# Blockwise causal attention and a gated FFN on one core: batch 2's q and k transposed between its v loads, its copies grouped, and one weight cast on VectorE

## The chip, the cores and the metric

The kernel runs on one core of one Trainium2 chip. The metric is the device time of one execution in microseconds; the median of several executions is compared. The profile is of one further execution, taken with the hardware profiler.

## The reference

Eight batches of eight heads, 576 positions, head width 64, all in float32. The attention is causal in blocks of 64 positions; its output, with the heads side by side, is the input of a gated feed-forward network (FFN).

```python
B, H, S, D = q.shape                      # 8, 8, 576, 64
scores = (1 / sqrt(D)) * (q @ k^T)
scores = where(row // 64 >= col // 64, scores, -1e9)
attn = softmax(scores)                    # over the keys
x = (attn @ v).transpose(0, 2, 1, 3).reshape(B * S, H * D)   # 4608 x 512
out = (relu(x @ w_gate) * (x @ w_val)) @ w_out               # d_ff = 1536
```

## The kernel before

Everything runs in bfloat16 with float32 sums. The 576 positions of a batch are split into 512 main positions and a tail of 64.

**Attention in rounds.** Round r is a pair of heads of one batch: batch r // 4, pair r % 4. A round multiplies keys with queries (`visit`, L378), exponentiates on ScalarE (L387, L393), sets the masked corners to zero by memset (`corners`, L686), multiplies with v for each head (`head_av`, `both_av`, L491), normalises on VectorE (L456, L457) and turns the result into xT, either by TensorE (`to_xT_pe`, L537, L538) or by a DMA transpose (`to_xT_dma`, L543). The tail of each batch is a round of its own kind (`tail_visit`, L412; `tail_av`, L471; its DMA transpose L485).

**The FFN as filler.** `ffn_gen` yields one matmul at a time: for each batch 96 products with w_gate and w_val (L568, with relu on ScalarE at L578 and the gating product hT on VectorE at L583) and 48 products with w_out (wo, L625, L645 to L659). One such matmul is one place, and 144 places are one batch. `run(base, events)` issues FFN matmuls up to each event's place and then the event. So events stand in a list, each with its place, and the order of every engine's instructions is the order in which the program issues them; there is no scheduler. Every engine and every DMA queue works in order. While the FFN of batch 0 runs (`run(0, ...)`) rounds 4 to 7 (batch 1) are interleaved with it; during the FFN of batch 1 (`run(144, ...)`) tail 0, rounds 8 to 11 (batch 2) and tail 1.

**Loading.** Float32 inputs go by DMA from the SP queue into a ring of ten `stage` buffers and are cast to bfloat16, mostly on GpSimd (called POOL in the profile): `cast_qk` (L168), `cast_v` (L181), `cast_v_chunks` (L189), `cast_tails` (L178), `cast_v_tail` (L195), weights in `cast_w` (L323). q and k must also be transposed. Batches 0 and 1 do that on TensorE (`pe_mains`, L238, copied out of the ffnp buffers of PSUM at L244; `pe_tails`, L256). Batches 2 and 3 do it by DMA: `transpose` (L209) turns one half (two pairs of heads) of q and of k into a `perm` buffer, and `unpermute` (L223) copies one pair from there into qTm (VectorE) and kTm (POOL), where `visit` reads it; their tails go by `transpose_tails` (L217). From batch 4 on, POOL's own DMA queue loads and casts in one step (`load_qkv`, L276).

**Buffers.** qTm, kTm, v_bf, qTt and kTt exist twice, by the parity of the batch, so batch 2 overwrites those of batch 0, which tail 0 reads last (kTm in its scores, v_bf in its products). The PSUM pool ffnp has three buffers; in the FFN of batch 0 the two output sums begun at place 96 hold two of them up to place 112.

Batch 2 before the change: its q and k are loaded first (`e2.load_qk`). At place 121 SP is given its v and its q and k tails (`load_2`), at 133 and 143 POOL casts a half of q and k and SP transposes it (`mains_2`), then come batch 2's v tail and batch 1's tails (`load_tails`). In the FFN of batch 1 the pairs are unpermuted at places 25, 45, 60 and 80, for rounds that begin at 41, 58, 75 and 92; `tails_2` at 32 casts both batches' tails on POOL and has SP transpose batch 2's, and `v_2` at 46 casts batch 2's v.

Of the kernel before, what the change touches and what calls it, by code (L numbers as in the profile page):

```python
# [17 lines left out]
def kernel(  # L18
# [88 lines left out]
    class Early:  # L107
# [46 lines left out]
        def load_tails(self, ts):  # L154
            both = new_stage(1024)
            for i, t in enumerate(ts):
                self.st["t", t] = both[0:64, 512 * i : 512 * i + 512]
                nc.sync.dma_start(
                    self.st["t", t].rearrange("p (h d) -> p h d", h=8),
                    (q, k, v)[t][self.b, :, 512:576, :].rearrange("h p d -> p h d"),  # L160
                )
# [156 lines left out]
    def load_w_out(i):  # L318
        return load_w(wo[i], moe_w_out, 512 * i)

    def cast_w(sts, eng):
        for dst, st in sts:
            eng(dst, st)  # L323
# [40 lines left out]
    def visit(r):  # L364

        b, hp = divmod(r, 4)
        at = attnT[r % 4]
        first = psum_sc.tile([128, 2, 512], FP, name="sc")
        second = psum_sc.tile([128, 2, 512], FP, name="sc")
        third = thirds()  # L370
        for c, hh in [(c, hh) for c in (2, 0, 1, 3) for hh in range(2)]:
            where = {
                0: first[:, hh, :],
                1: second[:, hh, 0:384],
                3: second[:, hh, 384:512],
                2: third[hh],
            }
            nc.tensor.matmul(  # L378
                where[c].rearrange("p (c n) -> p c n", n=128),
                kTm[b % 2][head_of(hh), c, hp, :],  # L380
                qTm[b % 2][head_of(hh), c:4, hp, :],
                start=True,
                stop=True,
            )

        def exp(sc, lo):
            return lambda: nc.scalar.activation(  # L387
                at[:, :, lo : lo + 512], sc, AF.Exp, scale=scale
            )

        def exp_third():
            for hh in range(2):
                nc.scalar.activation(  # L393
                    at[:, hh, 1024:1280], third[hh], AF.Exp, scale=scale
                )

        return exp_third, exp(first, 0), exp(second, 512)
# [44 lines left out]
    def corners(r, zero):  # L442

        at = attnT[r % 4]
        for lo, n in ((0, 512), (896, 128)):
            two = at[64:128, :, lo : lo + 2 * n].rearrange("p g (c n) -> p g c n", c=2)
            zero(two[:, :, :, 0:64])
# [52 lines left out]
    def head_av(r, hh):  # L500
        b, hp = divmod(r, 4)
        h = 2 * hp + hh
        at = attnT[r % 4]
        if hh == 0:
            xnats[r] = sb.tile([128, 4, 128], BF, name="xnat", bufs=3)
        xnat = xnats[r]
        if b > 0 or hh == 1:
            av = psum_ffn.tile([128, 4, 65], FP, name="ffnp")
        else:
            av = psum_one.tile([128, 4, 65], FP, name="one")  # L510
        products_with_v(b, h, at[:, hh, :], av)
        normalise(xnat[:, :, 64 * hh : 64 * hh + 64], av)

    def both_av(r):

        b, hp = divmod(r, 4)
        xnats[r] = sb.tile([128, 4, 128], BF, name="xnat", bufs=3)
        for hh in range(2):
            sc = psum_sc.tile([128, 2, 512], FP, name="sc")
            av = sc[:, 0, 0:260].rearrange("q (p e) -> q p e", e=65)  # L520
            products_with_v(b, 2 * hp + hh, attnT[r % 4][:, hh, :], av)
            normalise(xnats[r][:, :, 64 * hh : 64 * hh + 64], av)
# [160 lines left out]
    dve, act, pool = nc.vector.tensor_copy, nc.scalar.copy, nc.gpsimd.tensor_copy  # L683
# [7 lines left out]
    with tc.manual_schedule(engines={E.PE, E.DVE, E.Activation, E.Pool, E.SP}):  # L691
# [57 lines left out]
        e1, e2 = Early(1), Early(2)  # L749
        e1.load_qk(0, 4)  # L750
        ffn(23)
        w_out = [load_w_out(i) for i in range(2)]
# [11 lines left out]
        cast_w(w_out[0], pool)  # L764
        cast_w(w_out[1], pool)
        e1.cast_v(0, 4, pool)
        cast_w(w_out[2], pool)
        e1.cast_qk(4, 4, (pool, None))
        e1.cast_v(4, 4, pool)
        e0.cast_tails((pool, pool))  # L770
# [12 lines left out]
        def round_at(p, r, av, to_xT, after=(6, 13)):  # L783

            exps = []

            def begin():
                exps.extend(visit(r))
                exps[0]()
                exps[1]()  # L790

            return [
                (p, begin),
                (p + after[0], lambda: exps[2]()),
                (min(p + after[1], av[0] - 0.5), lambda: corners(r, zero_dve)),
                *(
                    [(av[0], lambda: both_av(r))]
                    if av[1] is None
                    else [(av[i], lambda i=i: head_av(r, i)) for i in range(2)]
                ),  # L800
                (to_xT[0], lambda: to_xT[1](r)),
            ]

        def tail_at(p, b, av):
            exps = []
            x = sb.tile([64, 512], BF, name="xtail", bufs=2)

            def begin():
                exps.extend(tail_visit(b))
                exps[0]()  # L810
                exps[1]()

            def end():
                tail_av(b, 1, x)
                tail_to_xT(b, x)

            return [
                (p, begin),
                (p + 6, lambda: exps[2]()),
                (av[0], lambda: tail_av(b, 0, x)),  # L820
                (av[1], end),
            ]
# [4 lines left out]
        early = {2: e2}  # L827

        def tails_2():
            e2.cast_tails((pool, pool))  # L830
            e2.transpose_tails()
            e1.cast_tails((pool, pool))
            e1.cast_v_tail(pool)

        def v_2():
            e2.cast_v_tail(pool)
            e2.cast_v_chunks(0, pool)
            e2.cast_v_chunks(1, pool)

# [9 lines left out]
        def mains_3(h0):  # L849
            early[3].cast_qk(h0, 4, (pool, pool))  # L850
            if h0 == 0:
                early[3].cast_tails((pool, pool))
# [7 lines left out]
        def un(b, hp, engs=(dve, dve)):  # L860
            return lambda: early[b].unpermute(hp, engs)

        def load_2():
            e2.load_v_chunks(0)
            e2.load_v_chunks(1)
            e2.load_tails((0, 1))

        def mains_2(h0):
            e2.cast_qk(h0, 4, (pool, pool))
            e2.transpose(h0 // 4)  # L870

        def load_tails():
            e2.load_tails((2,))
            e1.load_tails((0, 1))
            e1.load_tails((2,))

        events = round_at(96, 4, (112, 112.1), (116, pe_xT), (6, 11))
        events += round_at(104, 5, (120, 120.1), (127, pe_xT), (6, 15))
        events += round_at(126, 6, (138, 139), (146, pe_xT), (4, 9))
        events += round_at(137, 7, (148, None), (153, pe_xT), (3, 8))  # L880
        events += [
            (80, lambda: e1.cast_qk(0, 4, (None, dve))),
            (93, lambda: e1.pe_mains(0, (dve, act))),
            (95, lambda: e1.pe_mains(1, (dve, act))),
            (120.2, lambda: e1.cast_qk(4, 4, (None, act))),
            (121, load_2),
            (121.5, lambda: e1.pe_mains(2, (dve, act))),
            (123, lambda: e1.pe_mains(3, (dve, act))),
            (133, lambda: mains_2(0)),
            (142, lambda: e0.pe_tails((dve, act))),  # L890
            (143, lambda: mains_2(4)),
            (143, load_tails),
        ]
        run(0, events)
        events = tail_at(24, 0, (40, 44)) + tail_at(116, 1, (132, 136))
        for r, p in ((8, 41), (9, 58), (10, 75), (11, 92)):
            events += round_at(p, r, (p + 21, p + 25), (p + 25, to_xT_dma))
        events += [
            (100, lambda: e1.pe_tails((dve, act))),
            (20, lambda: store.pop()()),  # L900
            (32, tails_2),
            (25, un(2, 0, (dve, pool))),
            (45, un(2, 1, (dve, pool))),
            (46, v_2),
            (47, load_3),
            (60, un(2, 2, (dve, pool))),
            (62, lambda: mains_3(0)),
            (80, un(2, 3, (dve, pool))),
            (81, lambda: early[3].transpose(0)),
            (82, lambda: mains_3(4)),  # L910
            (101, lambda: early[3].transpose(1)),
# [6 lines left out]
        for b in range(3, B):  # L918
            events = tail_at(120, b, (136, 140))
# [43 lines left out]
```

## Time and profile before

| | us |
|---|---|
| Median of 4 runs (lowest, highest) | 373.39 (373.06, 375.13) |
| The profiled execution's own time | 376.17 |
| Its span, from the first to the last instruction | 374.3 |
| TensorE (PE) busy | 358.4, 96% of the span |
| VectorE (DVE) busy | 172.3, 46% |
| ScalarE (ACT) busy | 169.4, 45% |
| GpSimd (POOL) busy | 111.3, 30% |
| SP and ACT DMA queues, busy share of 16 engines | 44.0%, 7.9% |
| Mean granted TensorE clock | 0.991 of full speed |

Times in the profile are microseconds from the span's start. A line such as "PE one L378 <- POOL kTm L223: 3.3, 1, 3.3" says that TensorE's instructions of line 378 that write the tile `one` waited for POOL's writing of kTm at line 223, in total, how often, and the longest. In a timeline a line has its start, its length, engine, source line, operation, output<-input and shapes, and in brackets the idle time before it and what ended it. The stretches give for each window its length and each engine's busy time (with the number of instructions), then the granted clock, the DMA share and GB/s. Consecutive matmuls overlap in the trace, as their ends are modelled.

### The profile page before, as it was taken

To read this page: it belongs to the slowest core of one execution; us is meant where nothing else is said; L and a number is where in the kernel's file an instruction comes from. 1 tells how busy PE (TensorE), PEld (TensorE's weight loads), DVE (VectorE), ACT (ScalarE), POOL (GpSimd) and SP (SyncE) were. 2 spreads that over 40 slices of the span, in tenths; PEclk is the share of its full clock that TensorE was granted. 3 is DMA by queue.
4 is the path that set the end of the run, shared out by engine and by line. 5 is a ranking of instruction groups with operands and counts; after the bars stand their busy time and mean duration, and the time that the engine had idled before them with its cause. 6 is when DMAs were issued, how large, how long until landed. Compare 5 with 4: busy or idle time off the path is not lost.

```text
span 374.3 us, 7466 instructions
## 1 busy us (share of the span) xinstructions
PE 358.4 (96%) x2963; PEld 177.6 (47%) x2963; DVE 172.3 (46%) x398; ACT 169.4 (45%) x278; POOL 111.3 (30%) x142
## 2 busy tenths in 40 slices
PE   6899989869999999899999999999999999999996
PEld 2644544424555545344554545444544454444443
DVE  4744555434555553355335542554345444323432
ACT  4833755545426672355445534653366423302310
POOL 5765636257059940850048003000000000000000
PEclk9999999987999999999999999999999999999999
DMA  8999999959979999998669965957400330020004
GB/s 254 293 349 360 297 264 304 204 138 268 174 151 93 120 123 191 163 130 125 116 95 136 118 136 92 64 62 151 79 17 14 44 100 7 0 86 28 0 33 109
DMA packets 145188, 51.35 MB, mean 137 GB/s; under 512 B 124545, under 2 KB 139137, under 8 KB 145153
## 3 DMA queue, kind: packets, MB, share of 16 engines
q1 hardware_dynamic: 83616, 34.62, 44.0%
q0 software_dynamic: 56256, 7.08, 41.5%
q10 hardware_dynamic: 5280, 9.18, 7.9%
q8 instruction: 23, 0.38, 0.5%
q14 instruction: 13, 0.10, 0.1%
HBM read 37.75 MB, written 9.44 MB: 126 GB/s over the span
## 4 chain that ended last, share of the span: by engine, by line
PE 74%; DMA 15%; SPq 5%; POOL 2%; issue 1%; DVE 1%; ACT 1%; POOLq 0%
PE ffnp L568 42%; PE ffnp L625 21%; DMA stage<-in_moe_w_val_dram 5%; PE ffnp L491 4%; DMA stage<-in_moe_w_out_dram 4%; DMA stage<-in_q_dram 3%; PE sc L378 3%; DMA xT<-xnat 2%; PE ffnp L471 2%; SPq L139 2%; SPq L209 2%; PE one L378 1%; DMA stage<-in_k_dram 1%; PE sc L412 1%; POOL wo L323 1%
## 5 line engine op out<-in xcount | busy, mean ns | idle before, releaser
L583 DVE TENSOR_TENSOR hT<-gate_sb,ffnp 128x512 bf16<-128x512 bf16 x106 | 72.7, 686 | 91.9 <-PE ffnp L568 78.6
L578 ACT ACTIVATE gate_sb<-ffnp 128x512 bf16<-128x512 f32 x108 | 64.7, 601 | 105.3 <-PE ffnp L568 105.2
L568 PE MATMUL ffnp<-xT,wg 128*128 128x512 bf16 x384 | 104.8, 382 | 2.2 <-DMA xT<-xnat 1.4
L625 PE MATMUL ffnp<-wo,hT 128*128 128x512 bf16 (+1 forms) x444 | 102.0, 373 | 1.1 <-POOL wo L323 1.0
L568 PE MATMUL ffnp<-xT,wv 128*128 128x512 bf16 x376 | 101.4, 382 | 0.0
L568 PEld LDWEIGHTS <-wg 128*128 128x128 bf16 x432 | 40.5, 98 | 48.0 <-issue 4.9
L568 PEld LDWEIGHTS <-wv 128*128 128x128 bf16 x432 | 40.2, 98 | 46.4 <-issue 3.4
L625 PEld LDWEIGHTS <-hT 128*128 128x128 bf16 x444 | 40.7, 98 | 42.6 <-issue 1.9
L387 ACT ACTIVATE attnT<-sc 128x1024 bf16<-128x1024 f32 x56 | 57.0, 1040 | 0.0
L659 DVE COPY ob<-ffnp 128x512 f32<-128x512 f32 (+1 forms) x35 | 23.7, 676 | 40.5 <-PE ffnp L625 40.5
L276 POOL DMA_DIRECT2D v_bf<-in_v_dram x20 | 16.8, 880 | 69.0 <-PE ffnp L471 69.0
L491 PEld LDWEIGHTS <-attnT 128*128 128x128 bf16 x640 | 26.7, 99 | 14.7 <-DVE xnat L457 3.3
L456 DVE RECIPROCAL recip<-ffnp 128x4 f32<-128x4 f32 (+1 forms) x73 | 13.1, 179 | 39.6 <-PE ffnp L491 27.8
L393 ACT ACTIVATE attnT<-one 128x256 bf16<-128x256 f32 x28 | 10.7, 382 | 38.5 <-PE ffnp L378 35.6
L491 PE MATMUL ffnp<-v_bf,attnT 128*128 128x65 bf16 x570 | 27.0, 195 | 0.0
L457 DVE TENSOR_TENSOR xnat<-ffnp,recip 128x256 bf16<-128x256 f32 x57 | 24.2, 424 | 2.0
L378 PEld LDWEIGHTS <-kTm 64*128 64x128 bf16 x224 | 9.4, 95 | 19.9 <-issue 12.3
L433 ACT ACTIVATE attnTt<-one 64x256 bf16<-64x256 f32 x8 | 3.0, 377 | 33.0 <-PE ffnp L412 33.0
L378 PE MATMUL sc<-qTm,kTm 64*128 64x512 bf16 (+1 forms) x168 | 17.5, 312 | 0.0
L424 ACT ACTIVATE attnTt<-sc 128x1024 bf16<-128x1024 f32 x16 | 15.6, 1016 | 0.0
L276 POOL DMA_DIRECT2D k_bf<-in_k_dram x16 | 14.3, 930 | 1.5 <-DMA v_bf<-in_v_dram 1.1
L276 POOL DMA_DIRECT2D q_bf<-in_q_dram x16 | 14.4, 956 | 0.0
(86 smaller groups left out, 256.8 us busy)
## 6 DMA issues: line engine op xcount, KB each, us to landing
out_dram<-ob ACTq DMA_DIRECT2D x32, 256.0 KB, 2.4
stage<-in_moe_w_gate_dram SPq DMA_DIRECT2D x6, 512.0 KB, 9.0
stage<-in_moe_w_val_dram SPq DMA_DIRECT2D x6, 512.0 KB, 8.9
stage<-in_q_dram SPq DMA_DIRECT2D x6, 512.0 KB, 6.9
stage<-in_k_dram SPq DMA_DIRECT2D x6, 512.0 KB, 7.3
stage<-in_moe_w_out_dram SPq DMA_DIRECT2D x6, 512.0 KB, 8.8
stage<-in_v_dram SPq DMA_DIRECT2D x20, 128.0 KB, 5.7
stage<-in_v_dram SPq DMA_DIRECT2D x8, 256.0 KB, 6.7
```

The source lines that it names most:

```text
L276: nc.gpsimd.dma_start(dst, src[b, :, 128 * c : 128 * c + n, :].rearrange("h p d -> p h d"),)
L378: nc.tensor.matmul(where[c].rearrange("p (c n) -> p c n", n=128), kTm[b % 2][head_of(hh), c, hp, :], qTm[b % 2][head_of(hh), c:4, hp, :], ...
L387: return lambda: nc.scalar.activation(at[:, :, lo : lo + 512], sc, AF.Exp, scale=scale)
L424: return lambda: nc.scalar.activation(at[:, :, 2 * i : 2 * i + 2, 0:256], main[i].rearrange("p g (h n) -> p g h n", h=2), AF.Exp, scale=scale,
L456: nc.vector.reciprocal(recip, av[:, :, 64])
L457: nc.vector.tensor_tensor(out=out, in0=av[:, :, 0:64], in1=recip.to_broadcast([rows, n, 64]), op=AX.mult,)
L491: nc.tensor.matmul(av[:, p, :], at[:, col : col + 128], v_bf[b % 2][:, c, h, :], start=(p == 0), stop=(c == p), skip_group_check=True,)
L568: nc.tensor.matmul(to, (wg, wv)[t][f // 4][:, c, 128 * (f % 4) : 128 * (f % 4) + 128], x[:, c], start=(c == 0), stop=(c == 3),)
L578: nc.scalar.activation(gate_sb, gate, AF.Relu)
L583: nc.vector.tensor_tensor(out=h, in0=gate_sb, in1=val, op=AX.mult)
L625: nc.tensor.matmul(op, hT[f][:, 128 * s : 128 * (s + 1)], wo[f // 4][:, f % 4, n0:n1], start=(f == lo), stop=(f == hi - 1),)
L659: nc.vector.tensor_copy(ob, op)
```

## The change

Four things change, all in the order of issue; every matmul, cast and transfer remains.

1. Batch 2's loads on SP. `load_2` is gone. `mains_2` loads two of the four v pieces, casts a half of q and k and transposes it, so that SP has: v 0, v 1, transpose q and k of half 0, v 2, v 3, transpose half 1, and then batch 1's tails and batch 2's tails. `mains_2(0)` comes at place 128 instead of 133.
2. Batch 2's copies. The pairs are unpermuted at places 25, 28, 52 and 56. `tails_2` comes at place 60, with batch 1's tails cast ahead of batch 2's; with it the transposes of batch 2's tails stand behind batch 3's loads (place 47) in SP's queue.
3. The second half of wo's last third is cast by VectorE at place 112.3 instead of by POOL.
4. In the FFN of batch 0 the transposes of batch 1 and rounds 4 to 7 are up to 5 places later, and round 4's two products with v stand a place apart.

```diff
-        cast_w(w_out[2], pool)
+        cast_w(w_out[2][:1], pool)
...
         def tails_2():
+            e1.cast_tails((pool, pool))
+            e1.cast_v_tail(pool)
             e2.cast_tails((pool, pool))
             e2.transpose_tails()
-            e1.cast_tails((pool, pool))
-            e1.cast_v_tail(pool)
+            e2.cast_v_tail(pool)
 
         def v_2():
-            e2.cast_v_tail(pool)
             e2.cast_v_chunks(0, pool)
             e2.cast_v_chunks(1, pool)
...
-        def load_2():
-            e2.load_v_chunks(0)
-            e2.load_v_chunks(1)
-            e2.load_tails((0, 1))
-
         def mains_2(h0):
+            e2.load_v_chunks(h0 // 4)
             e2.cast_qk(h0, 4, (pool, pool))
             e2.transpose(h0 // 4)
 
         def load_tails():
-            e2.load_tails((2,))
             e1.load_tails((0, 1))
             e1.load_tails((2,))
+            e2.load_tails((0, 1))
+            e2.load_tails((2,))
...
-        events = round_at(96, 4, (112, 112.1), (116, pe_xT), (6, 11))
-        events += round_at(104, 5, (120, 120.1), (127, pe_xT), (6, 15))
-        events += round_at(126, 6, (138, 139), (146, pe_xT), (4, 9))
-        events += round_at(137, 7, (148, None), (153, pe_xT), (3, 8))
+        events = round_at(101, 4, (113, 114), (117, pe_xT), (6, 11))
+        events += round_at(108, 5, (120, 120.1), (128, pe_xT), (6, 11.5))
+        events += round_at(128.5, 6, (139, 140), (146, pe_xT), (4, 9))
+        events += round_at(138, 7, (148, None), (153, pe_xT), (3, 8))
         events += [
...
-            (93, lambda: e1.pe_mains(0, (dve, act))),
-            (95, lambda: e1.pe_mains(1, (dve, act))),
+            (96, lambda: e1.pe_mains(0, (dve, act))),
+            (98, lambda: e1.pe_mains(1, (dve, act))),
+            (112.3, lambda: cast_w(w_out[2][1:], dve)),
...
-            (121, load_2),
-            (121.5, lambda: e1.pe_mains(2, (dve, act))),
-            (123, lambda: e1.pe_mains(3, (dve, act))),
-            (133, lambda: mains_2(0)),
+            (123, lambda: e1.pe_mains(2, (dve, act))),
+            (125.5, lambda: e1.pe_mains(3, (dve, act))),
+            (128, lambda: mains_2(0)),
...
             (143, lambda: mains_2(4)),
             (143, load_tails),
...
-            (32, tails_2),
             (25, un(2, 0, (dve, pool))),
-            (45, un(2, 1, (dve, pool))),
+            (28, un(2, 1, (dve, pool))),
             (46, v_2),
             (47, load_3),
-            (60, un(2, 2, (dve, pool))),
-            (62, lambda: mains_3(0)),
-            (80, un(2, 3, (dve, pool))),
+            (52, un(2, 2, (dve, pool))),
+            (56, un(2, 3, (dve, pool))),
+            (60, tails_2),
+            (66, lambda: mains_3(0)),
```

## The prediction

> **What bounds the kernel now.** I read the page first, its slices and its chain of waits: TensorE is busy for 96% of the span, so time can only come from the stretches in which it is not, or in which its clock is low.
>
> ```profile
> PE   6899989869999999899999999999999999999996
> PEclk9999999987999999999999999999999999999999
> ```
>
> A slice is 9.36 us. Counted from 0, the holes lie in slices 5 (47 to 56 us), 7 and above all 8 (75 to 84 us), and the clock is low in slices 8 and 9. Then the waits of TensorE (how long in total, how often, the longest):
>
> ```profile
> PE one L378 <- POOL kTm L223: 3.3, 1, 3.3
> PE ffnp L679 <- POOL ident masks.py:199: 1.6, 1, 1.6
> PE ffnp L568 <- DMA xT<-xnat: 1.4, 2, 1.0
> PE ffnp L471 <- DVE hT L583: 1.1, 1, 1.1
> PE sc L335 <- DVE kTm L244: 1.1, 2, 0.9
> PE ffnp L625 <- POOL wo L323: 1.0, 2, 0.7
> ```
>
> The first is round 9 waiting for its keys. The stretches around it (TensorE's busy us after the length, the granted clock third from the end):
>
> ```profile
> 76.00:78.00 2.00, 2.00 (x11) 0.90 (x10) 1.73 (x5) 1.46 (x2) 0.00 (x0) 1.00 0.82 169
> 78.00:80.00 2.00, 0.68 (x4) 0.10 (x1) 1.51 (x2) 0.02 (x1) 1.18 (x2) 1.00 0.25 44
> 80.00:82.00 2.00, 0.05 (x2) 0.06 (x4) 0.00 (x0) 0.00 (x0) 2.00 (x4) 0.80 0.26 46
> 82.00:84.00 2.00, 2.00 (x11) 0.70 (x12) 0.00 (x0) 1.57 (x3) 2.00 (x3) 0.50 0.67 237
> 86.00:88.00 2.00, 2.00 (x14) 1.01 (x13) 1.07 (x3) 0.00 (x0) 1.82 (x3) 0.50 1.22 201
> 88.00:90.00 2.00, 2.00 (x13) 0.82 (x13) 1.39 (x5) 0.60 (x1) 1.91 (x4) 1.00 1.09 348
> ```
>
> So the wait is paid twice: 3.27 us of idleness, and then a half clock until 88. Why the keys were late stands in the timeline of GpSimd and of the SP queue:
>
> ```profile
> 78.82 0.61 POOL L178 CAST q_bt<-stage 64x512 bf16<-64x512 f32 x1 [4.19 <-DMA stage<-in_q_dram]
> 79.38 0.97 POOL L178 CAST k_bt<-stage 64x512 bf16<-64x512 f32 x1
> 80.30 0.61 POOL L195 CAST v_bf<-stage 64x512 bf16<-64x512 f32 x1
> 80.86 1.03 POOL L223 COPY kTm<-perm 128x512 bf16<-128x512 bf16 x1
> ```
>
> ```profile
> 66.78 1.62 SPq L209 DMA_TRANSPOSE perm<-q_bf  x1
> 68.50 1.73 SPq L209 DMA_TRANSPOSE perm<-k_bf  x1
> 73.70 0.63 SPq L158 DMA_DIRECT2D stage<-in_q_dram  x1
> ```
>
> Round 9's kTm copy (80.86) was ready to run at 73.5, but GpSimd works in order, and ahead of it stood the casts of batch 1's tails, whose load SP issued only at 73.70, behind the four transposes. And VectorE stood 3.34 us at its first qTm copy (71.38) until the first transpose landed at 71.36, with hT L583 behind it, for which TensorE waited 1.13 us at 72.62.
>
> **The change part by part.** All sums are against the profiled execution, with a span of 374.3 us; its own time was 376.17 and the median of the four timed runs is 373.39, so a saving is taken over onto the median unscaled.
>
> *Transposes earlier (SP).* Ahead of the first transpose now stand two of batch 2's four v loads instead of four and two tail loads. In the trace SP began the third v load at 60.67, and the casts that the transposes read ended at 59.95 (q) and 61.43 (k), so the new wait of SP for GpSimd is at most some tenths; behind it stand v's second half, the second pair of transposes and all tails, none of which anyone waits for soon. Landing: a transpose took 3.1 to 4.6 us from issue to landing, a v load of the same queue up to 8.8, so q's lands between 64 and 69.5. I take 67.3: the second v load landed at 66.44, and two transposes that followed each other landed 0.9 to 1.3 apart. k's then lands at 68.2, against 72.28. The second pair has the same bytes ahead of it as before, less two tail loads: about 72 and 73 instead of 73.6 and 74.8.
>
> *First wait (1.13 us).* VectorE reaches the two grouped copies at about 69 (68.04 before, and 0.8 from the retimed stretch below); perm has landed. Two copies of 0.59 end at 70.2, where the one before ended at 71.97, so hT is ready before TensorE asks: gain 1.13, between 0.5 (transpose landing at 69.5) and 1.13. The copies now run beside GpSimd's two kTm copies. The rows show what that costs: the VectorE copy of 78.96 took 0.91 instead of 0.59 beside a cast on GpSimd, and that engine's next cast 0.97 instead of 0.61. With 0.3 more per copy VectorE is free at 70.8, still in time. [...]
>
> *Second wait (3.27 us).* Round 9's kTm copy now stands right behind round 8's, both once tail 0's scores (67.2 to 67.9 before) are done: two copies of 1.06 end near 71, and round 9 asks near 77.5. Gain 3.27. What is next late: round 8's products with v, four FFN products after round 9's scores, near 79.3. They need both v casts (1.03 each), which GpSimd does once tail 0's products have read the old v (75.66 before, 1.1 less now) and v's second half has landed; the fourth v load landed at 68.54 and now has two more transposes ahead, so near 71. That gives 76.6 for the casts: 2.7 us of room. Rounds 10 and 11 need the copies of the second pair, done by 79, and ask at 83 and 88. Batch 1's tails are cast at 79 to 81 and asked for past 90. Batch 2's own tails and their transposes move behind batch 3's loads; their first reader is tail 2, at 111.58: free. SP, without these two transposes (2.00 and 1.18 at 75.86) ahead of batch 3's loads, begins them near 77.5 instead of 80.49; behind the two in their new place wait only xT transposes of batch 2, read after 144.
>
> *Clock.* From round 9's begin to round 10's TensorE took 7.91 us (81.95 to 89.86) and for the same work from round 10 to 11 5.42 (89.86 to 95.28). If no long idle stretch is left, 2.49 us come back; at most 3.0 (half of the 6.05 us after 81.95). I take 2.5, since round 10's own small waits (0.23 at 92.29) will be round 9's too. The clock fell at 81.18, 2.5 us into the pause, and stayed at 0.5 for 6.83 us; the 1.03 us of idleness between 46 and 48 did not lower it. [...]
>
> *The earlier stretch, retimed (38 to 56 us).* Transposes of batch 1 and rounds 4 to 6 move 2 to 5 FFN places later, into places where the two sums of the output occupy two of three ffnp buffers. Following the instruction order with the trace's durations: the first output product waits for the last hT (0.69 of VectorE), 0.45; the fourth group of transposes shares one buffer with the third and waits for its copy (0.69 plus hand-over), 0.9; round 4's third score 0.2; round 4's first product with v waits for the memset that now stands behind the second output copy (0.69 + 0.30), 1.0. That is 2.55, against 0.24 + 0.31 + 0.73 and some 0.3 of shorter pauses that the trace shows there and that go or coincide (wo's last loads land at 45.54 and 46.87 either way). The later pauses of the stretch (0.27, 0.17 and shorter ones) about keep their sum. So +0.8, between 0 and 2. The DVE cast of wo's last piece takes 0.69 (VectorE's cast of the same shape at 36.56), ends near 48.6, where its reader now comes at 48.8: no wait; behind it wait the two reciprocals of round 4, in the 0.8. GpSimd is relieved of 1.04 us that lay before a cast waiting for its load: nothing.
>
> *Sum.* 1.13 + 3.27 + 2.5 − 0.8 = 6.1: a span of 368.2, and 367.3 on the median. After 96 us TensorE hardly waits in the trace, so the rest shifts as a whole; the 1.4 us of waits for xT near 153 stay, within a microsecond either way.
>
> **The rivals.**
> [...]
> (2) A new wait takes the old one's place: round 8's v casts or the second pair of copies end 1.5 us after TensorE asks, and the clock falls again: 1.5 + 2.5 back, 371.3. Against it is the 2.7 us of room.
> (3) Slower: the transposes in the middle of SP's queue hold up v's second half. SP works in order, and this load decides from the moment that its cast ends after 79.3: each microsecond later is one of TensorE's, plus 2.5 for the clock. It turns the whole slower once the load lands past 82, 11 us later than I put it: with 5 us of wait 7.5 are paid against 6.1 won, 374.8; with 7, 376.8. For it: landings of up to 8.8 us in this stretch.
> (4) The wait goes but the earlier stretch costs more than its upper bound, 3 us or more, without the clock: 369.5.
>
> **How the numbers follow.** Forecast 0.74 (its own range 365.5 to 369), rival 1 0.07, rival 2 0.06, rival 3 0.06, rival 4 0.07. Low end: earlier stretch free, the whole 3.0 of the clock, a part of xT's waits: 365. High end: into rivals 1 and 4, 370.2. About 0.5% (1.9 us) is what a measurement of this kernel can tell from no change: faster than 371.5 are the forecast, rivals 1 and 4 and most of 2, 0.91; a mix of rivals 1 and 2 falls within, 0.04; slower 0.05.
>
> **What would show it.** Right: no wait of PE L378 on POOL kTm, the clock at 1.00 from 76 to 90, the first L209 issue near 61, kTm copies of rounds 8 and 9 adjacent near 70, round 9's scores near 78. The earlier stretch: TensorE at FFN place 128 some 0.8 us later than the 55.0 of before. Wrong: a wait of L491 on POOL v_bf, or a clock of 0.50 anywhere between 40 and 100.

## The result, and the profile after

No change. The changed kernel took 374.37 us (median of 36 runs, 372.69 to 376.01); in the same comparison the kernel before took 373.72 (55 runs). The ratio is 1.0012, with a 95% interval of 0.9999 to 1.0025. The profiled execution of the changed kernel took 374.92 us with a span of 372.8, 1.5 less than the span of before. The forecast was 367.3 us, and its range ended at 370.2.

The waits of TensorE after the change, largest first (total, how often, longest):

```profile
PE ffnp L568 <- DMA xT<-xnat: 3.7, 1, 3.7
PE ffnp L679 <- POOL ident masks.py:199: 1.6, 1, 1.6
PE sc L335 <- DVE kTm L244: 1.1, 2, 0.9
PE ffnp L491 <- DVE attnT L686: 0.8, 1, 0.8
```

The wait for round 9's kTm is gone, and so is that for hT behind the first copies. In first place stands a wait of about the same size that before did not have: an FFN matmul waits for xT, the transposed output of attention. The page's slices show where it is (a slice is 9.32 us):

```profile
PE   6899989999969999999999999999999999999996
PEclk9999999999988999999999999999999999999999
```

The hole of slice 8 is filled. A new one stands in slice 11 (102 to 112 us), with the low clock beside it, in slices 11 and 12. The stretches show both places (length, busy time of PE, PEld, DVE, ACT and POOL, then the granted clock, DMA share, GB/s):

```profile
78.00:80.00 2.00, 2.00 (x22) 0.93 (x20) 1.97 (x3) 1.43 (x3) 2.00 (x3) 1.00 0.76 78
86.00:88.00 2.00, 2.00 (x19) 1.05 (x18) 1.34 (x4) 1.36 (x2) 0.00 (x0) 1.00 1.12 335
106.00:108.00 2.00, 0.18 (x14) 0.15 (x5) 0.14 (x1) 1.36 (x3) 1.61 (x2) 1.00 1.19 215
108.00:110.00 2.00, 0.14 (x1) 0.10 (x1) 0.00 (x0) 0.00 (x0) 0.26 (x1) 0.68 0.87 96
110.00:112.00 2.00, 2.00 (x6) 0.64 (x5) 0.00 (x0) 1.51 (x2) 2.00 (x3) 0.50 0.37 65
114.00:116.00 2.00, 2.00 (x7) 0.78 (x6) 0.32 (x1) 0.50 (x1) 2.00 (x4) 0.61 1.83 117
```

Between 76 and 90 TensorE is busy at full clock, as forecast. Between 106 and 110 it stands, and the clock then stays at one half until about 115.6. The pattern of 78 to 88 of the kernel before has come back 28 us later. Who is late is seen in the SP queue of the changed kernel and in the matmul that waits:

```profile
94.31 1.22 SPq L543 DMA_TRANSPOSE xT<-xnat  x1
95.62 1.27 SPq L209 DMA_TRANSPOSE perm<-q_bf  x1
96.97 1.38 SPq L209 DMA_TRANSPOSE perm<-k_bf  x1
98.45 3.49 SPq L543 DMA_TRANSPOSE xT<-xnat  x2
102.03 1.26 SPq L209 DMA_TRANSPOSE perm<-q_bf  x1
103.39 1.58 SPq L209 DMA_TRANSPOSE perm<-k_bf  x1
105.06 2.33 SPq L543 DMA_TRANSPOSE xT<-xnat  x1
```

```profile
109.86 0.59 PE L568 MATMUL ffnp<-xT,wg 128*128 128x512 bf16 x1 [3.68 <-DMA xT<-xnat]
```

The last L543 is round 11's xT. It was issued at 105.06 behind batch 3's second pair of q and k transposes (102.03, 103.39) and landed at 109.82; TensorE went on at 109.86. Before the change the queue looked like this:

```profile
100.53 1.27 SPq L209 DMA_TRANSPOSE perm<-q_bf  x1
101.89 1.29 SPq L209 DMA_TRANSPOSE perm<-k_bf  x1
104.66 1.19 SPq L543 DMA_TRANSPOSE xT<-xnat  x1
```

Between 103.18 and 104.66 SP stood there and waited for its data, which VectorE finished at 104.63; after the change it was ready at 98.48, and SP came to it 6.6 us later. The last writing of round 11's xnat, before and after:

```profile
104.21 0.42 DVE L457 TENSOR_TENSOR xnat<-ffnp,recip 128x256 bf16<-128x256 f32 x1
98.06 0.42 DVE L457 TENSOR_TENSOR xnat<-ffnp,recip 128x256 bf16<-128x256 f32 x1
```

Before the change the transfer landed at 109.3. Its first reader is the fourth matmul of batch 2's FFN (place 291: the four matmuls of a sum read the four pairs of heads in turn, and round 11 is the last pair), which ran at 112.27: 3.0 us of room. After the change this matmul was due 6.1 us earlier, at 106.18 (109.86 less the wait), and SP, without a pause of over 1.8 us from 77 to 105, issued the transfer 0.4 us later than before; it landed 0.5 later. That is the wait: 6.1 − 3.0 + 0.5 = 3.6.

The ledger, by the start of scores in the two traces (us; "lead" is how much earlier the changed kernel is):

| | before | after | lead |
|---|---|---|---|
| tail 0 | 67.30 | 67.81 | −0.51 |
| round 9 | 81.95 | 78.26 | 3.69 |
| tail 1 | 102.69 | 96.38 | 6.31 |
| tail 2 | 111.70 | 105.55 | 6.15 |
| round 12 | 118.79 | 119.17 | −0.38 |
| round 16 | 153.57 | 152.77 | 0.80 |
| end of span | 374.3 | 372.8 | 1.5 |

So 6.15 us were won, and 6.53 were given back between tail 2 and round 12: 3.68 of waiting, and 2.85 of FFN work at half clock. Between round 12 and the end 1.9 came back, all of it from 145 to 162 us, where the changed trace has none of the 1.4 us of waits for batch 3's xT.

### The profile page after: what moved, and what is told of

It is laid out like the page before. It is cut to its first block, busy times and chain, and to the rows that moved or that the text cites. A ratio compares the mean times of both kernels' runs of the same rounds, so it can differ in the third digit from the quotient of the medians.

```text
span 372.8 us, 7469 instructions
## 1 busy us (share of the span) xinstructions
PE 358.4 (96%) x2963; PEld 176.9 (47%) x2963; DVE 173.6 (47%) x399; ACT 169.5 (45%) x278; POOL 111.6 (30%) x141
## 4 chain that ended last, share of the span: by engine, by line
PE 77%; DMA 16%; SPq 2%; ACT 1%; POOL 1%; issue 1%; DVE 0%; ACTq 0%; POOLq 0%
PE ffnp L568 43%; PE ffnp L625 22%; DMA stage<-in_moe_w_gate_dram 5%; PE ffnp L491 4%; DMA stage<-in_k_dram 3%; PE sc L378 3%; DMA stage<-in_moe_w_out_dram 2%; PE ffnp L471 2%; DMA stage<-in_v_dram 2%; SPq L139 2%; DMA perm<-k_bf 1%; PE one L378 1%; DMA xT<-xnat 1%; PE sc L412 1%; ACT attnTt L424 1%
```

## The experiments

Theory A: round 11's xT is late only because of its place in the SP queue, behind transposes that nobody needs so soon; take it out of there and the gain appears, up to the next thing that is late. Theory B: the transfers of this stretch are too many whatever their order, and TensorE waits near 106 us in any case. The kernels of one comparison ran with the kernel before on the same chip; each ratio is against that.

**e1: batch 3's second pair behind round 11's xT.**

```diff
-            (101, lambda: early[3].transpose(1)),
+            (117.5, lambda: early[3].transpose(1)),
```

> The changed kernel with one edit: batch 3's second pair of q/k transposes on SP (L209, issued at 102.03 and 103.39 in the changed kernel's profile) goes behind round 11's xT (issued at 105.06, landing at 109.82, TensorE asking at 106.2). Theory A (the 6.1 us are lost because round 11's xT stands on SP behind loads and transposes that nobody needs sooner, plus the half clock of 6.83 us): xT of round 11 lands near 106, the 3.68 us wait of L568 goes to under 1, tail 2 begins near 105.4 and the next place 6 us sooner. Then the next late thing is batch 3's xT (landing near 151 behind batch 4's transposes, which TensorE would now ask for near 146), so by A the whole is between 368 and 373, with a wait on xT near 146 to 150. Theory B (the DMA engines move so much there that order does not matter): the wait of about 3.7 us stays near 106, time as the changed kernel, 374.

371.98 us (before 373.47), ratio 0.9954 [0.9915, 0.9992]. Round 11's xT is now the last of three that SP issues in one row, at 101.64, and it landed at 104.47:

```profile
98.03 4.83 SPq L543 DMA_TRANSPOSE xT<-xnat  x3
102.96 1.26 SPq L209 DMA_TRANSPOSE perm<-q_bf  x1
```

From tail 2's scores to round 12 the trace has 7.09 us, exactly as in the kernel before (after: 13.62). The wait near 106 has gone with the order alone, so theory B falls. But the next thing is late at once, the xT of batch 3:

```profile
145.86 0.38 PE L568 MATMUL ffnp<-xT,wg 128*128 128x512 bf16 x1 [0.19 <-DMA xT<-xnat]
147.66 0.38 PE L568 MATMUL ffnp<-xT,wg 128*128 128x512 bf16 x1 [0.77 <-DMA xT<-xnat]
149.24 0.49 PE L568 MATMUL ffnp<-xT,wg 128*128 128x512 bf16 x1 [1.21 <-DMA xT<-xnat]
```

These are 2.2 us, and the clock fell beside them for 3.4 us (149.4 to 152.8).

**e2: round 11's xT by TensorE.** The DMA is left out, and four matmuls transpose instead.

```diff
-            events += round_at(p, r, (p + 21, p + 25), (p + 25, to_xT_dma))
+            events += round_at(
+                p, r, (p + 21, p + 25), (p + 29, pe_xT) if r == 11 else (p + 25, to_xT_dma)
+            )
```

> The changed kernel with round 11's xT made by TensorE's transposes and a VectorE copy instead of the DMA transpose; nothing else moves. Theory A: no wait for xT near 106 at all, clock 1.00 from 100 to 120, and the wait reappears at batch 3's xT (near 146), where 2 to 5 us of it are paid: 368 to 372. Theory B: TensorE waits as long for round 10's xT (landing at 103.5) or another DMA by 110: 374.

373.16 us, ratio 0.998 [0.9951, 1.0009]: by itself not to be told from before, and outside theory A's 368 to 372. The profiled run (371.96 us) has no wait near 106 either, as theory A says, and 1.6 us for batch 3's xT.

**e3: the copy alone.** The kernel before, in which only round 9's copies are moved.

```diff
-            (45, un(2, 1, (dve, pool))),
+            (28, un(2, 1, (dve, pool))),
```

> The kernel before with one part of the change: batch 2's second pair unpermuted at place 28 instead of 45, so its kTm copy stands on POOL ahead of the tails' casts; SP's queue as before. If the copies' order alone were what paid: the 3.27 us wait of round 9 and the half clock go, 368. By my reading of the traces the tails' casts (waiting for a load that lands at 78.7) still stand ahead of the two v casts on POOL, so round 8's products with v wait from about 80.5 to 83.4 instead, and the clock falls all the same: 372.5 to 374.

372.07 us, ratio 0.9967 [0.9941, 0.9993]: this one line gains about 1.2 us, where the whole change gains nothing. It moves the wait on to the casts of v:

```profile
PE ffnp L491 <- POOL v_bf L189: 2.0, 2, 1.3
```

The 2.0 us come as 1.34 and 0.67, and here the clock did not fall, which had been expected otherwise. In the listed runs it hardly fell at all: the mean granted clock was 0.999 or 1.000 in six of seven.

**e4: the xT of rounds 11, 13, 14 and 15 by TensorE.** As e2, and for batch 3:

```diff
-                events += round_at(p, r, (p + 20, p + 24), (p + 24, to_xT_dma))
+                events += round_at(
+                    p,
+                    r,
+                    (p + 20, p + 24),
+                    (p + 28, pe_xT) if b == 3 and i else (p + 24, to_xT_dma),
+                )
```

> The changed kernel with the xT of rounds 11, 13, 14 and 15 made by TensorE instead of by DMA (16 transposes more on TensorE, about 4 x 0.22 us). Theory A: both waits on xT (near 106 and near 146) are gone and what is left is at most the wait of round 16 for its DMA-transposed q and k (landing near 147.5): 367.5 to 370. Theory B: the time stays within 1 us of the changed kernel's, the waits moving to other transfers.

369.77 us (four runs), ratio 0.9906 [0.9884, 0.9928], as theory A says, and no wait for an xT in the whole trace. Its largest waits:

```profile
PE ffnp L679 <- POOL ident masks.py:199: 1.6, 1, 1.6
PE ffnp L238 <- ACT k_bf L168: 1.3, 1, 1.3
```

**e5: the early stretch alone.** The kernel before with parts 3 and 4 of the change (wo's last cast on VectorE, rounds 4 to 7 later), without parts 1 and 2.

```diff
-        events = round_at(96, 4, (112, 112.1), (116, pe_xT), (6, 11))
+        events = round_at(101, 4, (113, 114), (117, pe_xT), (6, 11))
...
+            (112.3, lambda: cast_w(w_out[2][1:], dve)),
```

> The kernel before with only batch 0's retimed early stretch and wo's last piece cast by VectorE; batch 2's loads and copies stay in their old places. Theory A (SyncE's order decides): the retiming makes TensorE 0.5 us later at place 128, and that lag is swallowed in front of tail 1, where TensorE waits for kTm anyway; span and time as before, 373 to 374.4 us, with the wait for kTm about 3.3 us minus nothing and the slow clock beside it. Theory B (the retimed stretch is worth something of its own, or costs it): 0.8 us or more slower, 374.5 or over, or 0.8 faster.

374.48 us (before 373.47), ratio 1.0004 [0.9972, 1.0036]. The time lies between the ranges of the two theories. Neither a gain nor a loss over 0.4% comes from there. Theory A's wait of 3.3 us did not come, as the waiting moved: for hT 2.5 us instead of 1.1, for kTm 0.7 instead of 3.3.

**e6: the change without the early stretch.** The changed kernel with those same lines as before.

```diff
-        events = round_at(101, 4, (113, 114), (117, pe_xT), (6, 11))
+        events = round_at(96, 4, (112, 112.1), (116, pe_xT), (6, 11))
...
-            (112.3, lambda: cast_w(w_out[2][1:], dve)),
```

> The changed kernel with the early stretch and wo's last cast as in the kernel before: only batch 2's loads and copies are moved. Theory A: TensorE is some 0.5 us earlier from place 128 on and waits that much longer for round 11's xT, which SyncE's queue sets: 3.7 to 4.3 us near 106 us and the slow clock there; time as the changed kernel's, 373.5 to 375. Theory B (the retiming costs what the move wins): the time falls by 1 us or more, to 373 or less, with no wait over 1 us near 106.

374.10 us, ratio 1.0016 [0.9983, 1.0048]; the wait is nearly as large as in the changed kernel, not larger as theory A had it, and in the profiled execution the clock did not fall. The time shows that the retiming did not eat the gain:

```profile
111.53 0.38 PE L568 MATMUL ffnp<-xT,wg 128*128 128x512 bf16 x1 [3.25 <-DMA xT<-xnat]
```

**e7: e2's edit on the kernel before.**

> The kernel before with round 11's xT transposed by TensorE instead of a DMA; nothing else. Theory A (round 11's xT is late only once the rest is 6 us earlier): nothing is won, 373.0 to 374.0 us, the wait for kTm and the slow clock beside it stay. Theory B (this transfer held up the kernel before as well, or taking a transpose from SyncE helps whatever else waits): 372.5 or less.

374.40 us, ratio 1.0007 [0.9983, 1.0032]: nothing won (the time is 0.4 above theory A's range). Round 11's xT held up nobody before.

**e8: e1's line and rounds 13 to 15 by TensorE, on the changed kernel.** Its diff is that of e1 with that of e4 for batch 3.

> The changed kernel with batch 3's second pair of q and k transposes put behind round 11's xT in SyncE's queue, and the xT of rounds 13 to 15 transposed by TensorE. Theory A: no wait for an xT anywhere, round 11's landing about 104.5 us; 368.5 to 370 us, at or below the run that gave the xT of rounds 11, 13, 14 and 15 to TensorE (369.8). Theory B (the later pair makes batch 3's own tails late): a wait for batch 3's q or k over 1 us, 371 or more.

370.50 us, ratio 0.9911 [0.9879, 0.9944]; no wait for an xT, and batch 3's later pair is not waited for. It lies 0.5 above the expected 370 and cannot be told from e4, whose interval overlaps.

**e9 and e10: why batch 3's xT is late.** In e1 these three took 9.4 to 10.3 us from issue to landing, where round 11's took 2.8. While they were queued, SP issued batch 4's two long transposes (L286, 5.1 and 6.1 us each), and GpSimd, which has nothing that holds it back, issued its loads of batch 5 from 123 us on. Both kernels start from e1 and put a memset of a later round on GpSimd ahead of those loads: round 15's in e9, round 16's in e10.

```diff
-                (min(p + after[1], av[0] - 0.5), lambda: corners(r, zero_dve)),
+                (
+                    min(p + after[1], av[0] - 0.5),
+                    lambda: corners(r, zero_pool if r == 15 else zero_dve),
+                ),
```

> The kernel of e1 (batch 3's second pair of transposes behind round 11's xT), and round 15's masking memset on GpSimd, so that GpSimd's loads of batch 5, which stand behind it, start near 135 us instead of 123. Theory A (the next late thing, batch 3's xT, lands 8 to 10 us after its issue because SyncE's long transposes of batch 4 and these loads share the DMA engines between 123 and 136): the two L286 transposes issue in under 4 us instead of 5.1 and 6.1, batch 3's xT land earlier, the wait of 2.2 us for them falls under 1 us; 369.5 to 371 us. Theory B (the waits come from SyncE's own order alone): the wait stays at 2 us or more, 371.5 to 372.5.

370.84 us (before 372.94), ratio 0.9941 [0.9914, 0.9969]. The loads began at 137.33, the long transposes took 4.8 and 5.2 us to issue, which is less relief than expected, and one wait of three is left, above the 1 us that theory A allowed. It is for round 15's xT, which met the loads:

```profile
150.73 0.38 PE L568 MATMUL ffnp<-xT,wg 128*128 128x512 bf16 x1 [1.19 <-DMA xT<-xnat]
```

e10 has 16 in place of 15 in that line, and batch 5's q and k loads at place 16 instead of 4 of batch 4's list.

> As e9, with the loads of batch 5 behind round 16's masking memset, near 149 us, so that no transfer of batch 3's xT meets them. Theory A: no wait for batch 3's xT over 0.3 us, 368.5 to 370.5 us, and the 6.1 us of the forecast are won but for a clock window. Theory B (SyncE's order alone, or the deferred loads are late for batch 5 instead): the wait of 2.2 us stays, or a new one for batch 5's q and k stands near 190 us; 371.5 or more.

373.63 us, ratio 1.0014 [0.9982, 1.0045]. Batch 3's xT landed 2.4 to 3.3 us after their issue and nobody waited for them: the collision with GpSimd's loads was what made them late. So theory A is right on batch 3, but not on the time. The collision is not gone. It now meets batch 4's xT, and the clock fell there too (189.6 to 193.0):

```profile
187.65 0.38 PE L568 MATMUL ffnp<-xT,wg 128*128 128x512 bf16 x1 [1.55 <-DMA xT<-xnat]
189.39 0.43 PE L568 MATMUL ffnp<-xT,wg 128*128 128x512 bf16 x1 [1.37 <-DMA xT<-xnat]
```

**e11: e10's deferral on the kernel before.**

> The kernel before with the loads of batch 5 behind round 16's masking memset, as in e10. Theory A: the 1.4 us of waits for batch 3's xT near 153 us go, and nothing else: 372 to 373 us. Theory B (the deferral is worth as much without the change, so it says nothing on where the change's gain went): 370.5 or less.

376.10 us, ratio 1.0082 [1.0052, 1.0111]: slower, by neither theory's numbers. Its waits for xT grew from 1.4 to 2.6 us, so on this kernel too the deferral only moves the collision (batch 3's xT landed within 2.6 us, and the waits now stand near 191 us). The runs also held 1.8 windows of half clock on average, the kernel before 0.9 (counted as under "The medians" below), which is worth 1.6 us. With the 1.2 us of waits that is most of the 3.2; the rest stays open.

**e12: rounds 13 to 15 by TensorE on the kernel before.** e4's diff for batch 3, alone.

> The kernel before with the xT of rounds 13 to 15 transposed by TensorE, as in e8, and nothing of the change. Theory A (the change's gain is real and comes out once no xT is late): this alone saves at most the 1.4 us of waits near 153 us, less some 0.7 us of transposes on TensorE (0.23 each by their places in e4's timeline); 372.3 to 374 us, against 370.5 for e8. Theory B (e8's time comes from these transposes alone, the change brings nothing): 371 us or less.

373.87 us (before 373.13), ratio 1.0023 [1.0000, 1.0047]. These transposes by themselves win nothing, so theory A holds. With the change and e1's line (e8) they come to 0.9911: the difference of the two ratios, 1.1% or 4.2 us, is what the change is worth once no xT is late. It goes through two comparisons and carries the error of both, about 0.4% of the time or 1.5 us. No run has e1's line on the kernel before; that it wins nothing there is argued from e7.

## Why the prediction was wrong

**The steps that held.** The first L209 was issued at 59.41 (forecast: near 61), q's transpose landed at 67.61 (67.3) and k's at 68.57 (68.2). Both of GpSimd's kTm copies stand together and its v casts begin at 75.28, in time. The lag of the early stretch was 0.49 at place 128 (forecast 0.8). The clock stayed at 1.00 from 76 to 90. The trace's lead at tail 2 is 6.15 against the forecast 6.1, though only against the one execution from which the forecast was sized (see below). The second pair landed at 73.71 and 74.52 instead of about 72 and 73, and nobody waited for it.

```profile
68.46 2.01 DVE L223 COPY qTm<-perm 128x512 bf16<-128x512 bf16 x2
...
68.73 2.68 POOL L223 COPY kTm<-perm 128x512 bf16<-128x512 bf16 x2 [5.32 <-DMA perm<-k_bf]
```

The copies cost more than I put down: VectorE's two took 2.01 us, 0.4 more per copy instead of 0.3, and all four 2.95 from the first start to the last end. By their rows of before they would have taken 2.39 beside each other without loss (GpSimd began 0.27 after VectorE), one after another 3.30 (two of 0.59 and two of 1.06). The 2.95 lie between the two, 0.35 below the second. It cost nothing: the next hT still ended at 71.80, and nobody waited.

**The step that failed** is the last of the sum: "After 96 us TensorE hardly waits in the trace, so the rest shifts as a whole". It rests on the sentence "behind the two in their new place wait only xT transposes of batch 2, read after 144". The number 144 counts places, not microseconds: batch 2's xT are read by the FFN of batch 2, which begins 144 places after that list's start (place 288 in all), at 110.83 us in the trace of before, and the sum never set that time against the landings. The last of them had 3.0 us of room, and a shift of 6.1 was laid on it. A transfer that nobody waits for in the trace has slack, and the slack has a size; I read the missing wait as free. The room could be read in the trace of before: landing 109.3, first use 112.27. With it the sum would have been 6.1 less 3.1 for the wait and some 2.5 for the clock again: about nothing, which is what was measured. The forecast also noted that two transposes of batch 2's tails move behind batch 3's loads; they took SP from 90.13 to 94.21 after the change, in the stretch whose end decides. What they cost by themselves no run separates.

**The rivals.** In the retimed stretch (38 to 56 us) the clock stayed at 1.00. Rival 2 had the right kind (a new wait in the old one's place and the clock with it: 371.3) but another place, round 8's v. Its place had been searched among the readers of the moved steps, not among everything that TensorE would ask for 6 us earlier. The mark for "wrong", a clock of 0.50 between 40 and 100, was also set too narrow: it came at 108.7.

**A term that was mis-sized, too.** From tail 0's to tail 1's scores the profiled execution of before took 35.39 us. Executions of the same program for this stretch are in e7, e11 and e12: 33.16, 32.83 and 32.91. After the change it is 28.57, and 28.16 to 28.52 in six of the seven kernels with the moved copies and loads (e8: 29.40). So the waits of this stretch, with the clock, were worth 4.7 to 5.0 us in those three traces and 7.2 in the one that I read; for kTm they waited 2.2 to 2.6 us instead of 3.27, and round 9 to round 10 took 6.66 instead of 7.91. That "a saving is taken over onto the median unscaled" was wrong: the profiled execution of before (376.17) was 2.8 above the median, and the waits that I meant to remove explain most of that. With 4.8 instead of 6.9, and 0.5 for the early stretch, 369 would have been the forecast (worked out after the result) for a kernel in which no xT is late. e4, which pays about 0.9 more for its transposes on TensorE (0.23 each in its timeline), measured 369.77.

**The medians.** The spans of the two profiled runs differ by 1.5 in favour of the change, the medians by 0.65 against it. The mean granted clock of each listed run, rounded to whole windows of 3.41 us at half clock (the spacing of the clock's changes in the traces, below; one lowers the mean by 0.0046), says how many it held, those at its start and end included. The kernel before had on average 0.96 in 91 runs, the changed one 1.44 in 36. Half of these 0.48 windows is 0.8 us, about the 0.65 of the medians. That a pause of 3.7 us takes the clock down more surely than one of 2.4 would explain it; I did not measure the two apart.

## What to carry to other kernels

Before a saving is carried to the end of the span, list what the bottleneck engine will ask for in the shifted stretch and give each transfer its room: first use less landing. The saving ends at the first whose issue does not move with it, above all one behind a busy in-order queue (here round 11's xT, which SP reached 6.6 us after its data was ready). And size a wait from more than one execution where there are any: the profiled one may be the extreme, and its own time above the median says so.

## What the runs showed of the hardware that was not expected

- The half clock does not follow from the length of a pause alone. It fell in pauses of 3.27 us (before) and 3.68 (after), for 6.8 us. It stayed at 1.00 in e6 through 3.25 us. In e7, e11 and e12 a pause of 2.2 to 2.6 was followed by 3.4 us of half clock. What fits all of these is how the pause lies on a grid that the traces show. In all fourteen, the clock's changes lie whole multiples of 3.413 us apart (in the changed kernel at 6.33, 108.73, 115.55 and 371.55: 30, 2 and 75 times 3.413). Where the clock fell in mid-kernel, TensorE had been busy for 0.6 to 1.4 us of the window before the fall. In e6 such a point (110.12, counted on from the change at 4.31 by 31 times 3.413) cuts the pause into 1.84 and 1.41 us, so that the two windows hold 1.57 and 2.00 us of work. The window before the fall in the kernel before and in the changed one, then e6's two:

```profile
77.77:81.18 3.41, 0.91 (x5) 0.19 (x2) 1.56 (x3) 0.25 (x1) 2.36 (x4) 1.00 0.29 49
105.31:108.72 3.41, 0.87 (x41) 0.73 (x41) 0.83 (x2) 1.56 (x3) 2.30 (x3) 1.00 1.15 189
106.71:110.12 3.41, 1.57 (x45) 0.93 (x43) 1.32 (x2) 1.55 (x3) 2.46 (x3) 1.00 1.10 252
110.12:113.53 3.41, 2.00 (x10) 0.93 (x10) 0.65 (x1) 1.51 (x2) 2.28 (x3) 1.00 0.47 89
```

Busy time does not tell it alone, and no run varies it by itself: in six traces (e2, e4, e8, e10, e11, e12) the clock also fell near 9 us, after windows with 1.9 to 2.1 us of work. What sets the half clock off was not shown.
- The start varies between executions of the same instructions: tail 0's scores began between 67.80 and 70.64 us in the changed kernel, e1, e4, e8 and e9, which do not differ up to there. In e9 (70.64) TensorE was slow for longer: at 16.22 us a pair of score matmuls (64x512) took 0.61 us, in the changed kernel 0.39 at 13.86. The listed clock does not count this (0.999 for e9). In e4 and e8 1.2 to 1.3 us went into a wait for k_bf (L168), of which the changed kernel had 0.3. Later stages can vary less: from tail 2's scores to round 12 it was 7.09 us in before, e1, e4, e8 and e9.
- The landing of a DMA transpose of one xT took from 2.4 us (e10) to 10.3 (e1). For batch 3's, putting off GpSimd's loads made the difference (2.4 to 3.3 in e10, 9.4 to 10.3 in e1). The issue of batch 4's two long transposes on SP (L286) took from 2.6 us (e11, with those loads put off) to 7.3 (e4).
